# Sparse attention and MoE: fewer weight operations in the first stage, the gate's low part on GpSimd for one chunk, V's middle rows in one transfer

## The chip, the cores and the metric

The kernel runs on one core of a Trainium2 chip. The metric is the device time of one execution in microseconds. A core has TensorE (PE in the profile; PEld is its weight load), VectorE (DVE), ScalarE (ACT), GpSimd (POOL) and SyncE (SP, which only issues transfers here). SP, ACT and GpSimd each have a queue of transfers of their own; 16 DMA engines serve them all.

## The reference

```python
# q, k, v: (4, 8, 768, 64); blocks of 32 rows, 24 of them; 3 sampled blocks for each
scores = scale * np.matmul(q, k.transpose(0, 1, 3, 2))
mask = np.abs(blk_i - blk_j) <= 1
mask = mask | (blk_i == 0) | (blk_j == 0) | (blk_i == n_blocks - 1) | (blk_j == n_blocks - 1)
for qb in range(n_blocks):
    for kb in sampled_blocks[qb]:
        mask[qb * block:(qb + 1) * block, kb * block:(kb + 1) * block] = True
scores = np.where(mask, scores, -1000000000.0)
...
attn = attn / (np.sum(attn, axis=-1, keepdims=True) + 1e-09)
attn_out = np.matmul(attn, v)                  # then laid out as x: (3072, 512)
h = x @ w_in                                   # (512, 2048)
g = h * (1.0 / (1.0 + np.exp(-1.702 * h)))
out = g @ w_out                                # (2048, 512)
```

All of it is float32.

## The kernel before

**Units and items.** Queries are taken in units of 64 rows. For each batch the first and the last block form a dense unit (all 768 keys, two items of four heads each); the other 22 blocks form eleven sparse units, and a pair of batches shares their keys and values. A sparse unit needs its neighbour blocks, block 0, block 23 and three sampled blocks per query block. Its values lie in two tiles: `vown` (128 rows for each of the two query blocks, gathered by an indirect DMA that GpSimd issues, with row numbers in `vidx`) and `vmid` (64 rows of the two query blocks themselves, 64 rows of the blocks 0 and 23, loaded by SP; a row of both batches is 4,160 bytes). `vmidof` remembers the batch pair whose edge rows a buffer holds, so that later only the first 64 rows are loaded. Entries of V have an `at`, their buffer (four in the first stage, then two), and are loaded by `load_v` once the entry that held the buffer before has had all its values issued.

**Order.** Everything is written out by hand: `run` opens with loads, `first` works through the items of units 0 to 8, then come the ticks. Items 0 to 3 are dense, 4 and 5 sparse, 6 to 9 dense, 10 to 12 sparse. An item goes through scores (L344 dense, L334 sparse), maximum on DVE, exponentials on ACT, transposes (L383) with copies on ACT, values (L421 dense, L412 sparse), normalisation and a turn (L445) into `x`. `loads` is called at the end of each item and asks for as many keys and rows as have a free buffer. In this stage the keys of sparse units are copied by GpSimd from the resident `kres` (L245, L249).

**The sampled blocks.** `indices`, a generator, turns the sampled blocks into `vidx`. It loads them twice on ACT's queue: one row (`sbr`) and a copy on all 128 partitions.

**The weights.** `weights` is a generator too: it turns the 32 loads of 512 KB of 64-bit words (`raw`) into high and low float32r parts (`win`, `wout`). Two calls open it; then each block takes four calls: a shift on DVE (with the request for a load some blocks ahead), an and-or on DVE and an absolute value on ACT for the next block, the low part of the block before on DVE, an or on DVE and a cast on ACT. The blocks of `w_out` end with a 256 KB store to `ws`. The first stage makes some calls between items, `tick` makes the rest: n0 after the first part of the attention, n1 inside `gate`, n2 at the end.

**The MoE.** A chunk is 512 tokens (8 units), and a tick is one of 16 feature blocks of a chunk: `up` (12 matmuls, L576 to L578), `gate` (tanh on ACT, product on DVE), `gate_hi` (cast on ACT to float32r), `gate_lo` (the rest, g - ghi, on DVE, at the start of the next tick), `down` for the tick before (16 matmuls; L627 and L628 take `ghi`, L623 at the end takes `glo`). Ticks 0 to 15 are the first chunk; in them the rest of the weights is made and the attention of the next units goes on. At even ticks there are an item's scores, at odd ones its transposes.

Of the kernel before, what the change touches and what calls it, by code (L numbers as in the profile page):

```python
# [9 lines left out]
F32 = mybir.dt.float32  # L10
# [8 lines left out]
P = 128  # L19
# [35 lines left out]
class Kernel:  # L55
# [3 lines left out]

    def __init__(self, ctx, tc, q, qd, kb, kT, v, vd, sb, w_in, w_out, out):  # L60
        self.tc, self.nc = tc, tc.nc
        self.q, self.qd, self.kb, self.kT, self.v, self.vd, self.sb = q, qd, kb, kT, v, vd, sb
        self.w64, self.out = (w_in.bitcast(I32), w_out.bitcast(I32)), out
# [75 lines left out]
        self.knext = self.vnext = 0  # L139
        self.early = True  # L140

# [7 lines left out]
    def indices(self):  # L149
# [15 lines left out]

        sb_i = take([2 * NB * NR]).bitcast(I32).rearrange("p (a b c) -> p a b c", a=NB, b=NR)
        nc.scalar.dma_start(out=sb_i.rearrange("p a b c -> p (a b c)"), in_=sb32.partition_broadcast(P))
        sbw = sb_i[:, :, :, 0]

        vblk = take([NB])  # L170
# [14 lines left out]
        make_identity(nc, self.ident)  # L185
        yield
        nc.vector.memset(vblk[:, 0:NB:NB - 1], 0.0)
        rr = take([NB, NR])
        d = take([NB, NR])
        ok = take([NB, NR])  # L190
        ne = take([NB, NR])
        nc.vector.tensor_copy(out=rr, in_=sbw)
        nc.vector.tensor_tensor(out=d, in0=rr, in1=qb.rearrange("p (a b) -> p a b", b=1).broadcast_to([P, NB, NR]), op=ALU.subtract)
# [67 lines left out]
    def load_v(self, e):  # L261
        nc, b, u, r = self.nc, e["b"], e["u"], e["at"]
        if u is None:
# [3 lines left out]
            return  # L267
        q0, v = 2 * u + 1, self.v[b // 2]
        if self.vmidof[r] != b:
            for h in range(2):  # L270
                r0 = BLK * (NB - 1) * h
                nc.sync.dma_start(out=self.vmid[r][UT + BLK * h:UT + BLK * (h + 1)], in_=v[r0:r0 + BLK])
            self.vmidof[r] = b
        nc.sync.dma_start(out=self.vmid[r][0:UT], in_=v[BLK * q0:BLK * (q0 + 2)])
        for j in range(2):
# [4 lines left out]
    def loads(self):  # L280
# [10 lines left out]
        def rows():  # L291
            n = self.vnext
            behind = self.vent[n]["behind"] if n < len(self.vent) else None
            if n == len(self.vent) or behind is not None and behind["values"]:
                return False
            self.load_v(self.vent[n])
            self.vnext += 1
            return True
# [300 lines left out]
    def gate_lo(self, m):  # L599
        if m not in self.g or len(self.g[m]) != 2:  # L600
            return
        g, ghi = self.g[m]
        glo = self.work.tile([P, CT], F32R, name="glo")
        self.nc.vector.tensor_tensor(out=glo, in0=g, in1=ghi.bitcast(F32), op=ALU.subtract)  # L604
        self.g[m].append(glo)
# [107 lines left out]
    def tick(self, m):  # L713

        n0, n1, n2 = 0, 0, 0
        if m < NF:
            heavy = any(part == self.scores for q in range(QT) for part, g in self.at.get(QT * m + q, ()))
            n0, n1, n2 = (2, 2, 4) if heavy else (2, 2, 2)

# [205 lines left out]
    def first(self):  # L925
# [7 lines left out]
        def weights(k):  # L933
            for _ in range(k):
                next(self.conv)
# [10 lines left out]
        def opening():  # L946
            a, b, c = items[:3]
            (least, *exps), (more, *other) = self.scores(a), self.scores(b)
            finish([least])
# [24 lines left out]
        for n, g in enumerate(items):  # L974
# [11 lines left out]
            if not sparse:  # L986
                finish(exps)
            weights(1 if sparse else 2)
            values(n - 2)
# [3 lines left out]
            if n >= len(items) - 3:  # L993
                values(n - 1)
            weights(0 if sparse else 2 if n == 3 else 1)
            pending.append(g)
            self.flush()
            self.loads()
        finish(self.transposes(items[-1]))
        while turns:  # L1000
# [100 lines left out]
```

## Time and profile before

| | |
|---|---|
| time, median of 3 runs | 737.5 us (736.21 to 739.92) |
| profiled execution | 734.55 us, span 732.8 us |
| TensorE busy | 712.3 us (97%), mean granted clock 0.993 |
| DVE, ACT, GpSimd busy | 451.0, 387.9, 62.3 us |
| moved by DMA | 123.23 MB, 168 GB/s on average |

The span runs from the first to the last instruction on the core; the time is a little longer. Busy shares are averages over stages that differ, so they are to be read by stretch. The first matmul of the first tick (L576) starts at 77.65 us: what lies ahead of it is called the first stage below.

### The profile page before, as it was taken

The numbers are of one execution on the slowest core, as the hardware profiler recorded it, in microseconds if no ns is written. First come the engines' busy times: TensorE is split into PE (matmuls) and PEld (weight loads), VectorE is DVE, ScalarE is ACT, GpSimd is POOL, SyncE is SP. The second block draws the span as 40 slices with busy tenths as digits, with TensorE's granted clock in tenths as the row PEclk, the third lists the DMA queues.
The fourth block names the chain that finished last, engine by engine and source line by source line (L and its number), as shares of the span: only waits on it lengthen the run. The fifth ranks groups of instructions, "written<-read, shape, count | busy, mean of one in ns | idle before, by whom it ended". The sixth has DMA issues, their size and how long they took to land.

```text
span 732.8 us, 18738 instructions
## 1 busy us (share of the span) xinstructions
PE 712.3 (97%) x7552; PEld 561.8 (77%) x7552; DVE 451.0 (62%) x839; ACT 387.9 (53%) x759; POOL 62.3 (9%) x105
## 2 busy tenths in 40 slices
PE   7987999999999999999999999999999999999996
PEld 4655788787778777877777777778778788888885
DVE  4676898899644544554454444554577877676552
ACT  4776767767455445554454445544334564545442
POOL 2236001011001111111011111100000000000000
PEclk9999999999999999999999999999999999999999
DMA  8999678888476666667565646721111311011542
GB/s 326 370 367 302 200 262 275 263 261 290 137 232 198 190 182 194 189 188 213 160 188 177 191 133 189 220 72 31 44 44 43 87 29 44 30 43 30 144 116 72
DMA packets 58872, 123.23 MB, mean 168 GB/s; under 512 B 7137, under 2 KB 24930, under 8 KB 58786
## 3 DMA queue, kind: packets, MB, share of 16 engines
q1 hardware_dynamic: 44928, 76.91, 34.5%
q0 software_dynamic: 6336, 23.43, 10.0%
q10 hardware_dynamic: 7522, 21.70, 9.1%
q8 instruction: 59, 0.97, 0.6%
q14 instruction: 27, 0.22, 0.1%
HBM read 111.53 MB, written 10.49 MB: 167 GB/s over the span
## 4 chain that ended last, share of the span: by engine, by line
PE 86%; DMA 6%; DVE 4%; ACT 2%; issue 1%; SPq 0%; ACTq 0%
PE banks L623 12%; PE banks L627 11%; PE banks L628 11%; PE banks L839 10%; PE banks L576 8%; PE banks L577 7%; PE banks L578 7%; PE banks L412 6%; PE banks L334 6%; PE banks L383 5%; DMA vown<-in_v_dram,vidx 2%; DMA vmid<-in_v_dram 2%; DMA raw<-in_moe_w_in_dram 2%; PE banks L445 1%; PE banks L344 1%; DMA kres<-in_kT_dram 1%
## 5 line engine op out<-in xcount | busy, mean ns | idle before, releaser
L627 PE MATMUL banks<-wout,ghi 128*128 128x512 f32 x384 | 151.4, 394 | 0.0
L628 PE MATMUL banks<-wout,ghi 128*128 128x512 f32 x384 | 149.7, 390 | 0.0
L623 PE MATMUL banks<-wout,glo 128*128 128x512 f32 x384 | 107.6, 394 | 1.2 <-DVE glo L604 1.0
L365 ACT ACTIVATE ex<-banks,nm 128x256 f32<-128x256 f32 x176 | 69.0, 478 | 74.4 <-DVE rg L428 74.0
L565 DVE TENSOR_TENSOR wout<-wst,wout 128x512 fp32r<-128x512 f32 x80 | 55.2, 690 | 69.3 <-ACT wout L564 68.7
L584 ACT ACTIVATE g<-banks 128x512 f32<-128x512 f32 x64 | 38.3, 599 | 86.9 <-PE banks L578 86.8
L627 PEld LDWEIGHTS banks<-wout,ghi 128*128 128x128 f32 x384 | 72.1, 188 | 15.9 <-ACT ghi L596 0.6
L623 PEld LDWEIGHTS banks<-wout,glo 128*128 128x128 f32 x384 | 70.7, 188 | 17.3 <-DVE glo L604 2.6
L628 PEld LDWEIGHTS banks<-wout,ghi 128*128 128x128 f32 x384 | 72.1, 188 | 14.9 <-DVE wout L496 0.5
L576 PE MATMUL banks<-x,win 128*128 128x512 f32 x192 | 78.7, 410 | 0.1
L389 ACT COPY pt<-banks 128x512 f32<-128x512 f32 x112 | 61.2, 589 | 30.2 <-PE banks L383 26.9
L577 PE MATMUL banks<-x,win 128*128 128x512 f32 x192 | 75.1, 391 | 0.0
L578 PE MATMUL banks<-x,win 128*128 128x512 f32 x192 | 75.0, 391 | 0.0
L276 POOL DMA_INDIRECT vown<-in_v_dram,vidx x44 | 42.4, 963 | 376.4 <-PE banks L412 363.5
L591 DVE SCALAR_TENSOR_TENSOR g<-g,banks 128x512 f32<-128x512 f32 x51 | 35.0, 687 | 58.8 <-ACT g L584 58.6
L596 ACT CAST ghi<-g 128x512 fp32r<-128x512 f32 x80 | 50.1, 626 | 37.4 <-DVE g L591 31.3
L351 DVE TENSOR_REDUCE mx<-banks 128x4 f32<-128x1024 f32 x44 | 53.7, 1220 | 25.6 <-PE banks L334 25.6
L383 PEld LDWEIGHTS banks<-ident,ex 128*128 128x128 f32 x436 | 49.9, 141 | 15.2 <-ACT pt L389 4.7
L383 PE MATMUL banks<-ident,ex 128*128 128x128 f32 x436 | 58.4, 276 | 2.0 <-ACT pt L389 1.4
L412 PEld LDWEIGHTS banks<-vown,pt 128*32 128x32 f32 x1408 | 42.2, 109 | 19.9 <-issue 13.4
L564 ACT CAST wout<-wst 128x512 fp32r<-128x512 f32 x80 | 50.5, 631 | 10.4 <-DMA wst<-ws 8.5
L604 DVE TENSOR_TENSOR glo<-g,ghi 128x512 fp32r<-128x512 f32 x80 | 54.8, 685 | 0.7
(123 smaller groups left out, 1148.8 us busy)
## 6 DMA issues: line engine op xcount, KB each, us to landing
wst<-ws SPq DMA_DIRECT2D x80, 256.0 KB, 2.7
kg<-in_kb_dram SPq DMA_DIRECT2D x126, 128.0 KB, 2.8
raw<-in_moe_w_in_dram ACTq DMA_DIRECT2D x16, 512.0 KB, 9.6
raw<-in_moe_w_out_dram ACTq DMA_DIRECT2D x16, 512.0 KB, 8.0
kg<-in_kb_dram SPq DMA_DIRECT2D x18, 384.0 KB, 4.8
vown<-in_vd_dram SPq DMA_DIRECT2D x8, 780.0 KB, 11.8
vmid<-in_v_dram SPq DMA_DIRECT2D x22, 260.0 KB, 5.6
qt<-in_q_dram SPq DMA_DIRECT2D x22, 256.0 KB, 2.8
```

The lines of the kernel that those rows point to most:

```text
L365: nc.scalar.activation(out=ex[:, cols], in_=sps[h][:, cols], func=AF.Exp, bias=un["nm"][:, c:c + 1], scale=SCALE)
L383: self.nc.tensor.transpose(ps[:, slot], g["ex"][h][:, k * P:(k + 1) * P], self.ident)
L389: self.nc.scalar.copy(out=pt, in_=ps)
L412: nc.tensor.matmul(sums[BLK * c:BLK * (c + 1), 2 * i + h], g["pt"][h][:, 2 * i + k, BLK * c:BLK * (c + 1)], src[:, at:at + DV], start=(k = ...
L565: self.nc.vector.tensor_tensor(out=t[:, DM:2 * DM], in0=w, in1=t[:, 0:DM].bitcast(F32), op=ALU.subtract)
L576: nc.tensor.matmul(h, wih[:, k], hi[:, k], start=(k == 0), stop=False)
L577: nc.tensor.matmul(h, wih[:, k], lo[:, k], start=False, stop=False)
L578: nc.tensor.matmul(h, wil[:, k], hi[:, k], start=False, stop=(k == NCT - 1))
L623: nc.tensor.matmul(o[n], glo[:, tk[n]], woh, start=False, stop=last)
L627: nc.tensor.matmul(o[n], ghi[:, tk[n]], woh, start=(f == 0), stop=False)
L628: nc.tensor.matmul(o[n], ghi[:, tk[n]], wol, start=False, stop=False)
L839: self.nc.tensor.matmul(bank, a[:, k], b[:, k], start=start and k + n == 0, stop=k == 1 and n == 2, skip_group_check=True)
```

## The change

- `weights`: in `first`, dense items after item 3 make one call and not three; in the first chunk the ticks without scores make seven calls and not six.
- `gate_lo`: for the 16 feature blocks of the first chunk the subtraction is issued on GpSimd and not on DVE.
- `held`: in the first stage no rows of V from entry 11 (`NV3`) on are loaded until the loop over the items has ended.
- `vm`: a second layout of V in DRAM holds the 128 middle rows of each unit together; where the edge rows are wanted too, one transfer of 128 rows takes the place of three.
- `indices`: the copy of the sampled blocks on all partitions is no longer loaded; a matmul of a row of ones with the row of sampled blocks makes it in bank 7, and ACT copies it out. The generator has one step more, taken between the scores of the first two items.

```diff
--- before.py
+++ after.py
@@ -57,9 +57,9 @@
-    def __init__(self, ctx, tc, q, qd, kb, kT, v, vd, sb, w_in, w_out, out):
+    def __init__(self, ctx, tc, q, qd, kb, kT, v, vm, vd, sb, w_in, w_out, out):
         self.tc, self.nc = tc, tc.nc
-        self.q, self.qd, self.kb, self.kT, self.v, self.vd, self.sb = q, qd, kb, kT, v, vd, sb
+        self.q, self.qd, self.kb, self.kT, self.v, self.vm, self.vd, self.sb = q, qd, kb, kT, v, vm, vd, sb
         self.w64, self.out = (w_in.bitcast(I32), w_out.bitcast(I32)), out
         self.ctx = ctx
         pool = self.pool = lambda name, bufs, **k: ctx.enter_context(tc.tile_pool(name=name, bufs=bufs, **k))
@@ -137,7 +137,7 @@
             e["at"] = (0, 2, 1, 3)[n % 4] if n < NV3 else (n - NV3) % RING
             e["behind"] = next((o for o in reversed(self.vent[:n]) if o["at"] == e["at"]), None)
         self.knext = self.vnext = 0
-        self.early = True
+        self.early = self.held = True
@@ -163,10 +163,11 @@
             at[0] += n
             return flat.rearrange("p (a b) -> p a b", a=shape[0]) if len(shape) == 2 else flat
-        sb_i = take([2 * NB * NR]).bitcast(I32).rearrange("p (a b c) -> p a b c", a=NB, b=NR)
-        nc.scalar.dma_start(out=sb_i.rearrange("p a b c -> p (a b c)"), in_=sb32.partition_broadcast(P))
-        sbw = sb_i[:, :, :, 0]
-
+        rr, d, both = take([NB, NR]), take([NB, NR]), take([2 * NB * NR])
+        ok, ne = (both[:, NB * NR * k:NB * NR * (k + 1)].rearrange("p (a b) -> p a b", a=NB) for k in range(2))
+        ones = both[0:1, 0:P]
+        nc.gpsimd.memset(ones, 1.0)
+        nc.vector.tensor_copy(out=d[0:1], in_=self.sbr)
         vblk = take([NB])
         first, second = slice(1, NB - 2, 2), slice(2, NB - 1, 2)
         nc.gpsimd.iota(vblk[3 * BLK:P, first], pattern=[[2, NU]], base=-NB, channel_multiplier=0,
@@ -184,12 +185,11 @@
         self.ident = self.bits.tile([P, P], F32, name="ident")
         make_identity(nc, self.ident)
         yield
+        spread = self.bank[7][:, 0:NB * NR]
+        nc.tensor.matmul(spread, ones, d[0:1].rearrange("p a b -> p (a b)"), start=True, stop=True)
+        nc.scalar.copy(out=rr, in_=spread.rearrange("p (a b) -> p a b", a=NB))
+        yield
         nc.vector.memset(vblk[:, 0:NB:NB - 1], 0.0)
-        rr = take([NB, NR])
-        d = take([NB, NR])
-        ok = take([NB, NR])
-        ne = take([NB, NR])
-        nc.vector.tensor_copy(out=rr, in_=sbw)
         nc.vector.tensor_tensor(out=d, in0=rr, in1=qb.rearrange("p (a b) -> p a b", b=1).broadcast_to([P, NB, NR]), op=ALU.subtract)
         nc.vector.tensor_tensor(out=ne[:, :, 0:2], in0=rr[:, :, 0:2], in1=rr[:, :, 1:3], op=ALU.not_equal)
         nc.vector.tensor_tensor(out=ne[:, :, 2], in0=rr[:, :, 0], in1=rr[:, :, 2], op=ALU.not_equal)
@@ -265,13 +265,9 @@
             nc.sync.dma_start(out=flat, in_=self.vd[b, e["i"]])
             e["vd"] = flat.rearrange("p (h k a d) -> p h k a d", h=2, a=2, d=DV)
             return
-        q0, v = 2 * u + 1, self.v[b // 2]
-        if self.vmidof[r] != b:
-            for h in range(2):
-                r0 = BLK * (NB - 1) * h
-                nc.sync.dma_start(out=self.vmid[r][UT + BLK * h:UT + BLK * (h + 1)], in_=v[r0:r0 + BLK])
-            self.vmidof[r] = b
-        nc.sync.dma_start(out=self.vmid[r][0:UT], in_=v[BLK * q0:BLK * (q0 + 2)])
+        q0, rows = 2 * u + 1, P if self.vmidof[r] != b else UT
+        self.vmidof[r] = b
+        nc.sync.dma_start(out=self.vmid[r][0:rows], in_=self.vm[b // 2, u, 0:rows])
         for j in range(2):
             nc.gpsimd.indirect_dma_start(
                 out=self.vown[r][:, j], out_offset=None, in_=self.v.rearrange("b s c -> (b s) c"),
@@ -290,6 +286,8 @@
         def rows():
             n = self.vnext
+            if self.held and n >= NV3:
+                return False
             behind = self.vent[n]["behind"] if n < len(self.vent) else None
             if n == len(self.vent) or behind is not None and behind["values"]:
                 return False
@@ -601,7 +599,7 @@
             return
         g, ghi = self.g[m]
         glo = self.work.tile([P, CT], F32R, name="glo")
-        self.nc.vector.tensor_tensor(out=glo, in0=g, in1=ghi.bitcast(F32), op=ALU.subtract)
+        (self.nc.gpsimd if m < NF else self.nc.vector).tensor_tensor(out=glo, in0=g, in1=ghi.bitcast(F32), op=ALU.subtract)
         self.g[m].append(glo)
     def down(self, m, part):
@@ -715,7 +713,7 @@
         n0, n1, n2 = 0, 0, 0
         if m < NF:
             heavy = any(part == self.scores for q in range(QT) for part, g in self.at.get(QT * m + q, ()))
-            n0, n1, n2 = (2, 2, 4) if heavy else (2, 2, 2)
+            n0, n1, n2 = (2, 2, 4) if heavy else (2, 2, 3)
         def run(n):
             for _ in range(n):
@@ -945,7 +943,9 @@
         def opening():
             a, b, c = items[:3]
-            (least, *exps), (more, *other) = self.scores(a), self.scores(b)
+            least, *exps = self.scores(a)
+            next(self.index)
+            more, *other = self.scores(b)
             finish([least])
             finish(exps)
             finish([more])
@@ -985,17 +985,18 @@
                 copies.append(self.turned(before, 2))
             if not sparse:
                 finish(exps)
-            weights(1 if sparse else 2)
+            weights(1 if sparse or n > 3 else 2)
             values(n - 2)
             finish(copies)
             if sparse:
                 finish(exps)
             if n >= len(items) - 3:
                 values(n - 1)
-            weights(0 if sparse else 2 if n == 3 else 1)
+            weights(2 if n == 3 else 0)
             pending.append(g)
             self.flush()
             self.loads()
+        self.held = False
         finish(self.transposes(items[-1]))
         while turns:
             finish(self.turn(turns.pop(0)))
@@ -1076,6 +1077,13 @@
     vs[:, :S, :, :, :D] = v.reshape(2, 2, S, H, D).transpose(0, 2, 1, 3, 4)
     vs[:, :S, :, :, D] = 1.0
+    vm = _np.empty((2, NU, 2 * UT, 2 * VROW), _np.float32)
+    for u in range(NU):
+        vm[:, u, :UT] = vs.reshape(2, SV, 2 * VROW)[:, BLK * (2 * u + 1):BLK * (2 * u + 3)]
+    for h in range(2):
+        r0 = BLK * (NB - 1) * h
+        vm[:, :, UT + BLK * h:UT + BLK * (h + 1)] = vs.reshape(2, 1, SV, 2 * VROW)[:, :, r0:r0 + BLK]
+
     def words(w):
         return _np.ascontiguousarray(w).view(_np.int64).reshape(NF, P, DM)
@@ -1086,6 +1094,7 @@
         "in_kb_dram": _np.ascontiguousarray(kb).reshape(P, 2, NB, 2 * NPAIR * BLK),
         "in_kT_dram": _np.ascontiguousarray(kT).reshape(B, P, NPAIR * S),
         "in_v_dram": vs.reshape(2, SV, 2 * VROW),
+        "in_vm_dram": vm,
         "in_vd_dram": vd.reshape(B, 2, P, VDROW),
         "in_sampled_blocks_dram": _np.ascontiguousarray(inputs["sampled_blocks"]),
         "in_moe_w_in_dram": words(inputs["moe_w_in"].reshape(NCT, P, NF, P).transpose(2, 1, 0, 3)),
```

## Rows read from the trace of the kernel before

**Rows 1.** Stretches: length, then busy us (and instructions) of each engine, clock, DMA share, GB/s.

```profile
30.00:40.00 10.00, 7.38 (x182) 5.33 (x163) 6.25 (x13) 6.77 (x14) 1.14 (x3) 1.00 1.03 315
...
40.00:50.00 10.00, 9.96 (x132) 6.04 (x132) 8.26 (x18) 6.23 (x12) 3.54 (x9) 0.83 1.03 414
...
60.00:70.00 10.00, 6.68 (x187) 4.96 (x183) 5.09 (x11) 5.01 (x12) 6.74 (x14) 1.00 1.03 265
...
77.65:192.00 114.35, 114.24 (x1230) 90.72 (x1230) 102.05 (x195) 78.13 (x156) 8.16 (x8) 1.00 0.80 253
192.00:520.00 328.00, 328.00 (x4241) 258.75 (x4240) 160.60 (x316) 160.57 (x347) 26.29 (x28) 1.00 0.57 171
```

**Rows 2.** What TensorE waited for from 0 to 75 us: total, times, longest.

```profile
PE banks L412 <- DMA vmid<-in_v_dram: 2.6, 1, 2.6
PE banks L344 <- DMA kres<-in_kT_dram: 2.4, 2, 2.1
PE banks L412 <- DMA vown<-in_v_dram,vidx: 1.8, 1, 1.8
...
PE banks L334 <- issue: 1.0, 1, 1.0
```

**Rows 3.** The chain that ended last, from 0 to 200 us: start, length, what.

```profile
25.93 12.87 DMA vmid<-in_v_dram
...
40.04 2.71 PE banks L344 x16
...
46.10 1.85 PE banks L344 x16
...
52.67 14.77 DMA vown<-in_v_dram,vidx
...
77.65 0.43 PE banks L576
...
115.19 0.91 PE banks L623 x4
```

**Rows 4.** Stretches, columns as in the first group, behind two of the waits.

```profile
40.00:44.00 4.00, 4.00 (x27) 2.08 (x26) 2.44 (x7) 1.00 (x3) 1.20 (x4) 0.57 1.04 415
66.00:68.00 2.00, 0.51 (x36) 0.51 (x40) 1.39 (x3) 1.65 (x5) 1.37 (x4) 1.00 1.05 272
```

**Rows 5.** Timeline of ACT and its queue: start, length, engine and line.

```profile
51.62 1.04 ACTq L478 DMA_DIRECT2D raw<-in_moe_w_out_dram  x1
...
56.92 0.33 ACTq L478 DMA_DIRECT2D raw<-in_moe_w_in_dram  x1
```

**Rows 6.** Timeline of GpSimd in the first stage.

```profile
53.61 2.66 POOL L245 COPY kg<-kres 128x256 f32<-128x256 f32 x6
...
62.04 0.94 POOL L276 DMA_INDIRECT vown<-in_v_dram,vidx  x1 [0.69 <-PE banks L421]
```

**Rows 7.** Timeline of SP's issues in the first stage.

```profile
23.31 2.58 SPq L272 DMA_DIRECT2D vmid<-in_v_dram  x2
```

**Rows 8.** The page's transfers: line, issues, KB each, median us from issue to landing.

```profile
wst<-ws SPq DMA_DIRECT2D x80, 256.0 KB, 2.7
...
vmid<-in_v_dram SPq DMA_DIRECT2D x22, 260.0 KB, 5.6
```

**Rows 9.** The page's groups: the low part on DVE, busy us and mean ns.

```profile
L604 DVE TENSOR_TENSOR glo<-g,ghi 128x512 fp32r<-128x512 f32 x80 | 54.8, 685 | 0.7
```

**Rows 10.** Timeline of ACT in the first chunk.

```profile
111.05 0.61 ACT L596 CAST ghi<-g 128x512 fp32r<-128x512 f32 x1
```

**Rows 11.** Timeline of DVE in the first stage.

```profile
55.14 0.87 DVE L496 TENSOR_TENSOR wout<-a,wout 128x512 fp32r<-128x512 f32 x1
...
65.35 1.01 DVE L353 TENSOR_SCALAR nm<-mx 128x4 f32<-128x4 f32 x1
```

**Rows 12.** Waits of all engines from 77 to 195 us.

```profile
ACT a L488 <- DMA raw<-in_moe_w_in_dram: 8.0, 6, 2.2
```

## The prediction

> **What bounds the kernel now.** I first read the stretches [rows 1]. From 77.65 us on, through the first chunk of the MoE and far beyond it, TensorE is busy without a gap (114.24 of 114.35 us, then 328.00 of 328.00): time can be won there by nothing but less TensorE work, and the change takes none away. Ahead of 77.65 us lies the attention stage, and its rows look different: DMA share 1.03 in each of the three stretches shown, TensorE busy only 7.38 of 10 us at 30 to 40 and 6.68 at 60 to 70, and a granted clock of 0.83 at 40 to 50. So the first 77 us are set by the transfers, the rest by TensorE.
>
> Next, TensorE's waits in that stage [rows 2]: 2.6 us for `vmid`, 2.4 us for `kres`, 1.8 us for the gathered `vown`, 1.0 us put to nothing ("issue"). The chain that ended last [rows 3] shows `vmid` and the gather from the other side: the last `vmid` transfer of the first sparse pair takes 12.87 us from issue to landing, and a gather 14.77 us, although each is a fraction of a megabyte. They are long because everything shares the 16 engines.
>
> A stall has a second price. Behind the 2.6 us wait the clock is 0.57 over 4 us [rows 4], so for most of them at the lower of its levels, 1.2 and not 2.4 GHz: the score matmuls of one item take 2.71 us there against 1.85 us a little later [rows 3]. That is (1 - 0.57) x 4 = 1.7 us of lost work. Around the 1.8 us wait, in which TensorE is busy 0.51 of 2 us, the clock stays at 1.00 [rows 4].
>
> **The change, part by part.**
>
> *Weight operations.* `weights` is a generator; two calls open it, then four make one weight block. The first stage now makes 1 call in the opening, 4 at item 3, 1 each at items 4 and 5, 1 each at items 6 to 9 (was 3 each), 1 each at items 10 to 12: 14 instead of 22. A block's load is asked for three blocks ahead in this stage, so 14 calls ask for 6 loads where 22 asked for 8. The two that leave the stage are those issued at 51.62 and 56.92 us [rows 5], 0.52 MB each; the one before them slides down by three items, because block 2 now begins at item 9, and the 0.26 MB store of `ws` that ends this block moves to item 12. So from 45 to 67 us the ACT queue carries some 1.3 MB less. Nothing changes before 45 us.
>
> *`held`.* The rows of entry 11 of V, two gathers, the first issued at 62.04 us [rows 6], and 64 rows of `vmid`, now wait until the loop over the items has ended. They are needed only at tick 4, some 28 us (4 x 114.35 / 16) into the first chunk, so the delay itself costs nothing; what they gave up is DMA time in the same stretch (rows are 4,160 bytes: 2 x 128 and 64 of them, 1.06 + 0.27 MB). No queue is held up by them: on GpSimd the key copies that came behind them come earlier.
>
> *V's middle rows.* Where a buffer first serves a batch pair, three transfers on SP (32, 32 and 64 partitions) become one of 128; the bytes are the same. SP was at the first two from 23.31 to 25.89 us [rows 7], and issued the third at 25.93 [rows 3]. In a backlogged queue an earlier issue alone wins nothing, since the bytes ahead are the same; what could win is the shape: 260 KB on 64 partitions land after a median 5.6 us, 256 KB of `wst` on 128 partitions after 2.7 us [rows 8]. So the landing at 38.80 us comes between 0 and 2.9 us earlier. I take 1.3 us, near the middle, as part of the 5.6 us is the queue and not the shape. The stall of 2.6 us becomes 1.3 us, shorter than the 1.8 us one that left the clock alone, so I also take the 1.7 us of clock as won; both may be nothing.
>
> *The sampled blocks.* A 72 KB broadcast load on ACT is replaced by one matmul with K = 1 and 72 columns, one ACT copy and a DVE cast of one row. The matmul goes between the first two items' scores, where TensorE waits up to 2.1 us for `kres` anyway [rows 2]; that wait is its cover, and without it it would cost some tenths of a us, once. The 72 KB at the 414 GB/s of 40 to 50 us [rows 1] are 0.2 us, which I take off the `kres` wait, with 0 and 0.5 us as bounds (small pieces may cost more than their bytes).
>
> *The gather's wait.* The 14.77 us gather [rows 3] starts when TensorE has left its buffer (the values of entry 5), so if TensorE comes 3 us earlier, so does the gather, and it must be through in 14.77 - 1.8 = 12.9 us to cause no wait. Against it ran the two weight loads, the store and later entry 11: the 22 us from 45 to 67 us carry 5.8 to 9.1 MB at the 265 to 414 GB/s of [rows 1]; without 1.3 to 2.6 MB of them, a seventh to two fifths, 14.77 us become 9 to 12.7. I take the 1.8 us as won. The 1.0 us "issue" [rows 2] may go too, but nothing shows what it waits for; I count none of it, and all of it for the upper bound.
>
> *The gate's low part.* Sixteen subtractions of 128x512 leave DVE, 685 ns each [rows 9], 11.0 us. GpSimd has no such row; a copy of 256 columns takes it some 0.44 us (2.66 us for six) [rows 6], so 512 columns are 0.8 to 0.9 us by columns, and twice that, 1.6 to 1.8 us, if the second input costs as much as the first. I take 1.6 us, bounds 0.8 and 2.0. TensorE needs the result at the end of the next tick: in one of the tighter ticks `ghi` is ready at 111.05 + 0.61 = 111.66 us [rows 10] and the low matmuls begin at 115.19 us [rows 3], so there are 3.5 us, and 1.6 us fit. GpSimd's queue holds only gathers beside it; `gate_lo` is issued ahead of the tick's gather, so it never stands behind a gather that waits for that tick's values.
>
> *DVE in the first chunk.* It is busy 102.05 of 114.35 us [rows 1]. Off: 11.0 us. On: the eight calls, two blocks of four operations of 512 columns at the same 0.69 us, 5.5 us. On top: what GpSimd's reads do to DVE operations with two SBUF inputs. While GpSimd copied [rows 6], such a subtraction took 0.87 us at 55.14 us [rows 11] in place of 0.685 [rows 9]: 0.185 us per copy of 0.44 us, so 16 x 1.6 x 0.185 / 0.44 = 10.8 us. Together 107.3 us, still under 114.35: no cost. Bounds: nothing, and the whole GpSimd time, 16 x 1.6 = 25.6 us, below as a rival. The Trainium skill, "SBUF — State Buffer", section "SBUF: two separate sides", says that the port pair which GpSimd shares with DVE is an exclusive lock, held for a whole instruction, against DVE operations with two SBUF inputs too. By that rule DVE would stand for each whole subtraction; the row above shows a partial delay. The same skill, "GPSIMD Engine Reference", section 3.1, gives 2.6 cycles per element at 1.2 GHz for two inputs; 512 elements would be an estimated 1.1 us, less than what I take.
>
> *Lead of the weights.* A tick pair now makes 8 + 7 calls (was 8 + 6), so 14 + 8 x 15 = 134 = 22 + 8 x 14: both end the chunk level. A block is ready four calls or more before the matmul that reads it, two for `wout` at the last ticks, as before; at tick 8 the lead falls from 11 calls to 7. No cost. ACT takes two blocks more in the chunk, 78.13 of 114.35 us now [rows 1], no bound.
>
> **Sum.** 1.3 (stall for `vmid`) + 1.7 (clock) + 1.8 (gather) + 0.2 (`kres`) = 5.0 us; bounds 0 and 2.6 + 1.7 + 2.8 + 0.5 = 7.6 us. The profiled execution took 734.55 us (span 732.8 and 1.75 around it), which becomes 729.6. It is 3 us under the median of the three runs, 737.5, for which the time is 732.5 us.
>
> **The rivals.**
>
> *The relief is hidden.* The first 45 us of transfers are the same bytes, so the `vmid` stall may stay, and with it the clock: then only 1.8 + 0.2 us come, perhaps less where another wait takes the gather's place: 735.5 to 737. For it: DMA share 1.03 at 30 to 40 us [rows 1]. Against it: the narrow transfers of `vmid` land late for their size [rows 8]. Chance 0.30.
>
> *ACT stalls in the first chunk.* Two weight loads more are asked for there. ACT already waits for `raw` in the chunk, 8.0 us in 6 waits, the longest 2.2 us [rows 12], and TensorE doesn't feel it. If two more such waits came at a bad place and passed through to TensorE, 4.4 us of the 5.0 would go: 736.9. Chance 0.06.
>
> *DVE becomes the bound (slower).* Should a GpSimd subtraction stop DVE for its whole length g, DVE's work is 102.05 - 11.0 + 5.5 + 16 g. It passes 114.35 us at g = 1.11 us; it eats the 5.0 us at g = 1.42; at g = 2.0 the chunk is 14.2 us longer, and the time is 737.5 - 5.0 + 14.2 = 746.7 us. For it: beside GpSimd's copies an operation on four columns took DVE 1.01 us [rows 11]. Against it: the 0.185 us above. Chance 0.08. By the rule of "SBUF — State Buffer" named above this is the case to expect; only the partial delay of the row keeps its chance low.
>
> **How the numbers follow.** The forecast (a gain of 3.7 to 7.6 us) has 0.56. A measurement of this kernel can tell about 0.5% from no change, 3.7 us. Faster 0.56; same 0.30 + 0.06 = 0.36; slower 0.08. For 8 in 10 the range runs from 729.0 (8.5 us won, the bound and some 1 us for what one measurement differs from the next) to 738.0: it leaves out the slower rival and a few hundredths at the lower end.
>
> **What would show it.** Right: the first up-projection begins near 72.7 us instead of 77.65; TensorE's wait for `vmid` is under 1.8 us and the clock at 40 to 44 us is 1.00; no wait for the gather; the chunk behind stays about 114.3 us long, with TensorE gapless and DVE near 107 us. Wrong: the wait for `vmid` and the low clock are still there, or a new wait stands at another item of the first stage; a GpSimd subtraction over 3.5 us, or a DVE without idle time and TensorE waiting for `glo`, `g` or `wout`.

## The result, and the profile after

The changed kernel takes 743.08 us (median of 10 runs, 741.32 to 745.80), the kernel before 736.38 us (median of 10 runs): 1.0088 times as long, 95% interval 1.0069 to 1.0106. It is slower by 0.9%; forecast was 732.5 us in a range of 729.0 to 738.0.

The stretches say where the time went. Columns as in [rows 1]; the first fence is the changed kernel, cut at its first up-projection (72.25 us) and at the one of tick 16, the second the kernel before, cut at the same places of the program.

```profile
0.00:72.25 72.25, 62.97 (x1194) 45.29 (x1194) 44.68 (x109) 47.44 (x88) 27.07 (x70) 1.00 0.88 331
72.25:198.02 125.77, 117.18 (x1227) 89.75 (x1221) 106.67 (x182) 80.38 (x159) 30.84 (x24) 0.99 0.72 238
198.02:740.50 542.48, 534.46 (x5146) 427.55 (x5140) 301.23 (x534) 260.65 (x513) 26.23 (x28) 1.00 0.42 128
```

```profile
77.65:190.00 112.35, 112.24 (x1222) 89.05 (x1221) 100.16 (x190) 77.76 (x155) 8.16 (x8) 1.00 0.80 255
190.00:732.80 542.80, 534.50 (x5141) 427.15 (x5140) 301.08 (x534) 260.64 (x513) 26.29 (x28) 1.00 0.43 128
```

The first stage is 77.65 - 72.25 = 5.4 us shorter (5.3 by the timeline of TensorE, in which the first matmul of the kernel before starts at 77.58), the forecast was 5.0. The rest behind the first chunk is the same (542.48 and 542.80). The first chunk, forecast unchanged, is 125.77 us long instead of 112.35: 13.4 us more. In 8.6 of them TensorE is idle (125.77 - 117.18); it is also busy for 4.9 us more, of which some 1.5 are the low clock shown below (0.50 over 3 us) and the others were not traced. What it waits for there, in the second fence, it did not wait for before; the first fence is the first stage and answers to [rows 2].

```profile
PE banks L381 <- ACT pt L387: 2.4, 5, 0.9
PE banks L342 <- DMA kres<-in_kT_dram: 1.7, 3, 0.8
PE banks L342 <- ACT ex L366: 1.2, 1, 1.2
...
PE banks L410 <- DMA vmid<-in_vm_dram: 0.6, 1, 0.6
```

```profile
PE banks L626 <- DVE wout L494: 5.0, 4, 1.8
PE banks L381 <- ACT ex L363: 2.9, 1, 2.9
PE banks L576 <- DVE win L494: 0.2, 1, 0.2
```

In the first stage the wait for `vmid` fell from 2.6 to 0.6 us, the one for the gather is gone, and the clock stands at 1.00 over the whole stage, at 40 to 44 us too (first row below), where [rows 4] had 0.57. In the chunk there are two kinds of wait. One is late weights: the second matmul of a down-projection (L626) wants the low half of `wout`, and DVE has not made it. The other is a single stall of 2.9 us, in front of the transposes of tick 5, with the clock at 0.50 behind it (second row).

```profile
40.00:44.00 4.00, 2.75 (x83) 1.74 (x83) 2.08 (x8) 2.46 (x4) 1.87 (x5) 1.00 1.01 413
```

```profile
109.00:112.00 3.00, 3.00 (x9) 2.27 (x8) 2.73 (x4) 2.69 (x7) 1.37 (x1) 0.50 0.37 112
```

What stands ahead of the single stall is in ACT's timeline (start, length, engine and line, and the idle time before it): a load of weights is asked for at 98.52 us, ACT stands still for 3.95 us for it, and behind that operation in its queue are the exponentials (L363) that the transposes need.

```profile
98.52 0.39 ACTq L476 DMA_DIRECT2D raw<-in_moe_w_in_dram  x1
...
106.00 0.72 ACT L486 ACTIVATE a<-raw 128x512 f32<-128x512 f32 x1 [3.95 <-DMA raw<-in_moe_w_in_dram]
106.57 0.51 ACT L363 ACTIVATE ex<-banks,nm 128x256 f32<-128x256 f32 x1
```

The kernel before has such a load at the same tick, asked for at 103.06 us and used 7.4 us later, after ACT has stood still for 1.75 us. There the exponentials (L365) are ahead of the operation that waits, and TensorE doesn't feel it. The view puts the end of that wait down to a transfer of keys, so the load itself may have landed a little earlier.

```profile
103.06 0.34 ACTq L478 DMA_DIRECT2D raw<-in_moe_w_in_dram  x1
...
106.20 1.57 ACT L365 ACTIVATE ex<-banks,nm 128x256 f32<-128x256 f32 x4 [1.38 <-DVE rg L428]
...
110.48 0.67 ACT L488 ACTIVATE a<-raw 128x512 f32<-128x512 f32 x1 [1.75 <-DMA kg<-in_kb_dram]
```

The last view is of GpSimd and DVE around two of the moved subtractions. DVE's shift of 512 columns (L524) takes 0.42 us as a rule; beside GpSimd's subtraction it takes 1.36 us, and it ends some 0.3 us after GpSimd does (110.63 + 1.61 = 112.24; 111.17 + 1.36 = 112.53). The other subtractions look alike: wherever a shift began beside one, it ended 0.28 to 0.29 us after GpSimd, and a subtraction of DVE's own ended 0.55 us after it.

```profile
110.63 1.61 POOL L602 TENSOR_TENSOR glo<-g,ghi 128x512 fp32r<-128x512 f32 x1 [8.29 <-ACT ghi L594]
117.18 1.62 POOL L602 TENSOR_TENSOR glo<-g,ghi 128x512 fp32r<-128x512 f32 x1 [4.94 <-ACT ghi L594]
```

```profile
111.17 1.36 DVE L524 TENSOR_SCALAR a<-a 128x512 int32<-128x512 int32 x1
...
114.71 0.42 DVE L524 TENSOR_SCALAR a<-a 128x512 int32<-128x512 int32 x1
...
117.73 1.36 DVE L524 TENSOR_SCALAR a<-a 128x512 int32<-128x512 int32 x1
```

### The profile page after: what moved, and what is told of

The parts are those of the page before. It is cut to its first block, busy times and chain, and to the rows that moved or that the text cites. A ratio compares the mean times of both kernels' runs of the same rounds, so it can differ in the third digit from the quotient of the medians.

```text
span 740.5 us, 18757 instructions
## 1 busy us (share of the span) xinstructions
PE 714.6 (97%) x7554; PEld 562.6 (76%) x7554; DVE 452.6 (61%) x823; ACT 388.5 (52%) x760; POOL 84.1 (11%) x122
## 4 chain that ended last, share of the span: by engine, by line
PE 68%; DVE 4%; ACT 3%; issue 1%; DMA 1%; ACTq 0%
PE banks L621 10%; PE banks L625 9%; PE banks L837 9%; PE banks L626 9%; PE banks L574 6%; PE banks L575 5%; PE banks L576 5%; PE banks L410 5%; PE banks L332 4%; PE banks L381 4%; PE banks L443 1%; DVE gs L760 1%; DMA raw<-in_moe_w_in_dram 1%; ACT ghi L594 1%; DVE wout L563 1%
## 5 line engine op out<-in xcount | busy, mean ns | idle before, releaser
L626 PE MATMUL banks<-wout,ghi 128*128 128x512 f32 x384 | 150.4, 392 | 5.1 <-DVE wout L494 5.0
L363 ACT ACTIVATE ex<-banks,nm 128x256 f32<-128x256 f32 x176 | 69.0, 479 | 78.0 <-DVE rg L426 53.9
L626 PEld LDWEIGHTS banks<-wout,ghi 128*128 128x128 f32 x384 | 72.2, 188 | 21.8 <-DVE wout L494 7.4
L625 PEld LDWEIGHTS banks<-wout,ghi 128*128 128x128 f32 x384 | 72.1, 188 | 15.7 <-ACT ghi L594 0.4
L349 DVE TENSOR_REDUCE mx<-banks 128x4 f32<-128x1024 f32 x44 | 53.7, 1220 | 24.4 <-PE banks L332 24.3
L410 PE MATMUL banks<-vown,pt 128*32 128x65 f32 x1408 | 50.3, 221 | 1.9 <-ACT pt L387 1.0
```

The lines of the kernel that those rows point to most:

```text
L363: nc.scalar.activation(out=ex[:, cols], in_=sps[h][:, cols], func=AF.Exp, bias=un["nm"][:, c:c + 1], scale=SCALE)
L410: nc.tensor.matmul(sums[BLK * c:BLK * (c + 1), 2 * i + h], g["pt"][h][:, 2 * i + k, BLK * c:BLK * (c + 1)], src[:, at:at + DV], start=(k = ...
L625: nc.tensor.matmul(o[n], ghi[:, tk[n]], woh, start=(f == 0), stop=False)
L626: nc.tensor.matmul(o[n], ghi[:, tk[n]], wol, start=False, stop=False)
```

## The experiments

All times are medians, against runs of the kernel before on the same chip. "Calls" are the weight calls of the first stage and of a tick pair; "low part" is the engine of the gate's subtraction in the first chunk; the last three columns are read from each trace's timeline of TensorE: the start of the first up-projection, the length of the first chunk from there to tick 16 (112.35 us in the kernel before), and the longest distance between the scores (32 matmuls) of two even ticks up to tick 14, which is 14.3 us in the kernel before. The pair of ticks 14 and 15, 14.3 to 18.7 us long, is left out of that column. The runs e1 to e4 were made on one chip, e5, e6, e8 and e9 on a second, e7 and e10 to e12 on a third, e13 and e14 on a fourth.

| kernel | calls | low part | us | before | ratio (95%) | first tick | chunk | longest pair |
|---|---|---|---|---|---|---|---|---|
| the change | 14, 15 | GpSimd | 743.08 | 736.38 | 1.0088 (1.0069 to 1.0106) | 72.25 | 125.77 | 19.8 |
| e1_lo_dve | 14, 15 | DVE | 739.93 | 737.26 | 1.0038 (1.0018 to 1.0058) | 72.49 | 122.00 | 18.6 |
| e2_weights_old | 22, 14 | GpSimd | 730.53 | 737.26 | 0.9899 (0.9879 to 0.9918) | 72.34 | 114.20 | 15.8 |
| e3_both_undone | 22, 14 | DVE | 730.20 | 737.26 | 0.9898 (0.9879 to 0.9916) | 72.45 | 112.92 | 14.3 |
| e4_before_lo_pool | 22, 14 | GpSimd | 736.71 | 737.26 | 0.9989 (0.9976 to 1.0002) | 78.38 | 113.27 | 15.2 |
| e5_first18 | 18, 15 | DVE | 733.83 | 737.31 | 0.9962 (0.9940 to 0.9985) | 71.24 | 119.28 | 15.9 |
| e6_first22_15 | 22, 15 | DVE | 735.19 | 737.31 | 0.9964 (0.9945 to 0.9983) | 70.14 | 123.63 | 20.0 |
| e8_exps_first | 14, 15 | DVE | 746.69 | 737.31 | 1.0128 (1.0095 to 1.0162) | 69.71 | 132.32 | 20.9 |
| e9_first14_16 | 14, 16 | DVE | 731.03 | 737.31 | 0.9915 (0.9886 to 0.9945) | 69.81 | 117.02 | 15.8 |
| e12_change_16 | 14, 16 | GpSimd | 734.11 | 737.07 | 0.9962 (0.9948 to 0.9976) | 70.36 | 120.52 | 15.9 |
| e13_noloads14 | 14, 15 | DVE | 733.33 | 738.18 | 0.9933 (0.9906 to 0.9959) | 70.30 | 118.90 | 16.2 |
| e14_noloads22 | 22, 15 | DVE | 729.90 | 738.18 | 0.9890 (0.9864 to 0.9916) | 69.84 | 115.64 | 15.5 |
| e7_vm_only | 22, 14 | DVE | 730.86 | 737.07 | 0.9915 (0.9899 to 0.9932) | 73.35 | 114.86 | 15.5 |
| e10_held_only | 22, 14 | DVE | 735.94 | 737.07 | 0.9992 (0.9978 to 1.0007) | 77.22 | 112.05 | 14.3 |
| e11_index_only | 22, 14 | DVE | 736.63 | 737.07 | 0.9992 (0.9977 to 1.0007) | 76.36 | 114.86 | 14.6 |

**The two parts that touch the chunk, each alone and both undone.** Theory LOCK blames GpSimd's subtractions, theory LEAD the moved weight calls.

e1_lo_dve:

```diff
-        (self.nc.gpsimd if m < NF else self.nc.vector).tensor_tensor(out=glo, ...)
+        self.nc.vector.tensor_tensor(out=glo, ...)
```

> The changed kernel with the gate's low part back on DVE; the eight weight calls stay in the first chunk. Theory LOCK (a GpSimd subtraction stops DVE's operation beside it until it is done, and the weights come late by that): the first chunk falls from 125.8 us back to 113 to 116 us, the first stage stays near 72.3 us, so the time is about 12 us under the changed kernel, 729 to 733 us, below the kernel before. Theory LEAD (the eight moved calls alone leave the weights too little lead, and ACT waits for their loads): DVE has 11 us more to do here, the chunk stays at 122 us or more, the time at 740 to 748 us.

e2_weights_old:

```diff
-            n0, n1, n2 = (2, 2, 4) if heavy else (2, 2, 3)
+            n0, n1, n2 = (2, 2, 4) if heavy else (2, 2, 2)
...
-            weights(1 if sparse or n > 3 else 2)
+            weights(1 if sparse else 2)
...
-            weights(2 if n == 3 else 0)
+            weights(0 if sparse else 2 if n == 3 else 1)
```

> The changed kernel with the weight calls of the kernel before (22 in the first stage, 8 and 6 in the tick pairs); the low part stays on GpSimd. LOCK: DVE is stopped as often as in the changed kernel, so its operations beside GpSimd still take 1.0 to 1.6 us and the chunk stays near 120 us or more: 736 to 742 us. LEAD: the weights have their old lead of 15 calls, which hides the stops: the chunk is 112 to 115 us, the first stage between 72.3 and 77.7 us: 731 to 736 us.

e3_both_undone has both diffs.

> Both undone; what stays of the change is V's middle rows in one transfer, the held rows and the sampled blocks by a matmul. Both theories: the chunk is that of the kernel before, 112 to 114 us. What it tells is where the first stage's 5.4 us came from: if from the wider transfer and the opening, it stays under 74 us and the time is 731 to 734 us; if from the two weight loads less, it goes back to 76 to 78 us and the time to 735 to 737 us.

e4_before_lo_pool is the kernel before with the first diff turned round (DVE to GpSimd).

> The kernel before with nothing changed but the low part of the first chunk on GpSimd. LOCK alone: the chunk grows by several us, 740 to 748 us in all. LEAD: the old lead hides it, the time is that of the kernel before within 2 us.

LOCK as the main cause fell: with the low part back on DVE the kernel is still slower than the one before, and with the weight calls back it is 1.0% faster, whichever engine does the low part (e2, e3); on the kernel before GpSimd's part can't be told from nothing (e4). The moved calls cost 739.93 - 730.20 = 9.7 us. GpSimd adds some 3 us, but only where they have been moved (743.08 against 739.93). And the moved calls bought nothing: on the chip of e1 to e4 the first tick starts at 72.49 us with 14 calls (e1) and at 72.45 us with 22 (e3), on the second chip at 69.71 and 69.81 us with 14 (e8, e9) and at 70.14 us with 22 (e6), on the fourth at 70.30 and 69.84 us (e13, e14). Between these groups the same first stage differs by up to 2.8 us. Whether that is the chip was not tested; but a difference between medians from two chips can hold as much that has nothing to do with the edit, so the chunks are compared beside them below.

**Lead in microseconds.** From the timelines one can read when DVE ended the low half of `wout` of a feature block and when TensorE came to the down-projection that reads it. The second matmul of a down-projection is the first that wants the low half; without a wait it starts 0.23 us after the first one. From DVE's end to that moment, in us (negative: TensorE waited):

```
feature block    0     2     4     6     8    10    12    13    14
before         28.8  11.6   9.9   5.4   5.5   3.3   2.2  -0.1   0.5
e3  (22, 14)   27.2  11.6   9.6   5.4   4.5   3.3   1.1  -0.7   0.5
the change      4.3   2.2   3.1   0.6  -0.6  -1.5   0.2  -0.3  -1.5
e1  (14, 15)    4.3   2.7   3.0   1.9   0.5  -0.9   0.5  -0.2  -1.2
e9  (14, 16)    4.3   3.6   3.4   3.4   3.4   3.4   3.4   4.8   4.4
e6  (22, 15)   25.8  11.6  13.9  11.5   8.7   7.8   4.5   7.1   5.7
```

The kernel before runs its lead down to zero just at block 13: it had none to give away. With eight calls less zero is reached at block 8 (the change) or 10 (e1), and from there on TensorE goes at the pace of the weights. One such wait, in TensorE's timeline of the changed kernel:

```profile
169.77 0.50 PE L626 MATMUL banks<-wout,ghi 128*128 128x512 f32 x1 [1.77 <-DVE wout L494]
```

The next four kernels vary the lead, and try to take away the long pair at ticks 4 and 5.

e5_first18 is e1 with `weights(0 if sparse else 2 if n == 3 else 1)` at the end of an item, so one call more in each of four items.

> Low part on DVE, 18 weight calls in the first stage (two in each dense item after item 3), 15 in a tick pair. LEAD in us: a call of lead is worth about 1 us; 14 calls (e1) ran out of slack at tick 8 to 10, 22 calls (e3) at tick 13; 18 with 15 a pair keep a lead of 8 or 9 calls, so TensorE doesn't wait for wout: 730 to 733 us. A rival, RATE (15 calls a tick pair are more than DVE and ACT can do, whatever the lead): tick pairs of 15 us and more from about tick 6 on, 735 to 740 us.

e6_first22_15 is e3 with `(2, 2, 4) if heavy else (2, 2, 3)`, one call more in a tick pair.

> Low part on DVE, 22 weight calls in the first stage, and 15 in a tick pair, one more than the kernel before has. LEAD: never short, 729 to 731 us, as with 22 and 14 or up to 0.6 us better. RATE: the pairs are too full, 733 to 738 us.

e9_first14_16 is e1 with:

```diff
-            n0, n1, n2 = (2, 2, 4) if heavy else (2, 2, 3)
+            n0, n1, n2 = (2, 2, 4)
```

> Low part on DVE, 14 weight calls in the first stage as in the change, and 16 in a tick pair, so that the lead stays at some 8 calls and doesn't fall to 2. LEAD: the late ticks don't wait for wout any more; what is left is the stall at ticks 4 and 5 by a load: 733 to 736 us. RATE: 16 calls are worse than 15, 739 to 745 us.

e8_exps_first is e1 with:

```diff
-        if not turning:
+        if not turning and not (m < NF and heavy):
             self.flush()
```

> The changed kernel with the low part on DVE (739.9 us), and in the ticks with scores the weights' ACT operations left over from the tick before come behind the exponentials and not ahead of them. If the tick pair of 18.6 us (ticks 4 and 5) comes from ACT standing at an absolute value that waits for its load, with the exponentials behind it (theory RAW, beside LEAD): this pair falls to 14.3 to 15 us, the later ones stay long, 735 to 737 us. If the pair is long for want of lead: no change, 738 to 741 us.

With 16 calls in a pair the slack stays at 3.4 us or more, no `wout` is late, and the time is 731.03 us: LEAD holds. The stall that was expected to stay at ticks 4 and 5 did not come: that pair is 15.7 us long. RATE as it was put, 739 to 745 us, falls, since the densest pairs are the best of the three kernels with 14 calls. But fuller pairs are not free: e9's chunk is 117.02 us long where e3's is 112.92, and the two times agree only because e9's first tick, on the other chip, starts 2.6 us earlier. In e5, which was expected at 730 to 733 us and takes 733.83, no `wout` is late either; its TensorE waits for `g`, DVE's product, in the last ticks (first fence). And e6 was expected at 729 to 731 us and takes 735.19: it has slack in plenty, waits for `g` too, and still has one pair of 20.0 us. So LEAD isn't all. e6's TensorE and ACT show the same stall as the changed kernel, at the same place (second and third fence):

```profile
PE banks L574 <- DVE g L589: 2.9, 2, 1.6
```

```profile
PE banks L381 <- ACT ex L363: 2.7, 1, 2.7
PE banks L574 <- DVE g L589: 2.4, 2, 1.3
```

```profile
97.56 0.39 ACTq L476 DMA_DIRECT2D raw<-in_moe_w_in_dram  x1
...
104.90 0.67 ACT L486 ACTIVATE a<-raw 128x512 f32<-128x512 f32 x1 [3.83 <-DMA raw<-in_moe_w_in_dram]
105.47 0.46 ACT L363 ACTIVATE ex<-banks,nm 128x256 f32<-128x256 f32 x1
```

e8 was a miss: it shortened that pair only from 18.6 to 16.6 us, and, as the weights' ACT operations now came later, TensorE waited for the high half of `wout` too. At 746.69 us it is the slowest of all.

```profile
PE banks L625 <- ACT wout L501: 3.9, 2, 3.1
PE banks L626 <- DVE wout L494: 3.6, 4, 2.4
PE banks L574 <- ACT wst L587: 2.3, 2, 1.2
```

**Is it the loads?** In e13 and e14 no weights are loaded behind the first stage:

```diff
                 f, i = todo[k]
+                if not self.early:
+                    tiles[k] = {"raw": tiles[4 + k % 2]["raw"]}
+                    return
```

> Low part on DVE, 14 calls in the first stage, 15 in a tick pair (739.9 us), but after the first stage the weights' loads are left out: the later blocks are made again from two tiles that are already there, so the weights are wrong and 26 loads of 512 KB are missing. Two causes are told apart. If the long tick pair 4 and 5 (18.6 us) is ACT waiting for a load, it falls to 14.3 to 15 us, while the late ticks still wait for wout (lead): 734 to 736.5 us. If the pair is long for want of lead, it stays above 17 us, and the time within 2 us of 739.9. If the waits for wout too come from the loads, all goes: under 732 us.

> The same omission with 22 calls in the first stage and 15 in a tick pair (735.2 us; 24 loads missing, wrong weights). This kernel has lead enough, and one long pair, 20.0 us at ticks 4 and 5. If this is the load: all pairs near 14.3 us and 728 to 731 us. If it is where 15 calls a pair fall in the tick, whatever they wait for: it stays, 734 us or more.

Without loads the pair at ticks 4 and 5 is 14.8 us long in e13 and 14.7 us in e14. e14, which has its lead, is at 729.90 us, 5.3 us under e6. e13, which hasn't, is at 733.33 us, 6.6 us under e1, and its waits for `wout` stay:

```profile
PE banks L629 <- DVE wout L497: 3.7, 3, 1.5
PE banks L381 <- ACT ex L363: 0.3, 1, 0.3
```

So there are two losses, and taking away the loads leaves the other. The lead's size can be read off on one chip: 733.33 - 729.90 = 3.4 us, and 118.90 - 115.64 = 3.3 us by the chunks. That of the late loads is less sure. By medians it is 6.6 us, but e13 ran on another chip than e1, and in the two traces 2.2 us lie ahead of the first tick, where the kernels are the same; by the chunks it is 122.00 - 118.90 = 3.1 us, which is what the stall itself comes to: the wait for the exponentials falls from 2.1 to 0.3 us, and 1.4 us of clock (0.72 over 5 us in e1, from 108 us on) come back. From e14's chunk to e3's another 115.64 - 112.92 = 2.7 us are left, with neither loads nor a short lead: what remains of the edit there is the fifteenth call in each pair. That is no more than two traces can differ by: e7 and e11 have the weight calls of the kernel before and chunks 2.5 us longer.

**The first stage, part by part, on the kernel before.** e7_vm_only has the diff's lines of `vm` and no others, e10_held_only those of `held`, e11_index_only those of `indices` and the `next(self.index)` between the first scores.

> The kernel before with V's middle rows in one transfer and nothing else. Of the first stage's some 5 us that stay when the weight calls go back (e3), the wider transfer should bring the wait for vmid (2.6 us) and the low clock behind it (1.7 us): the first stage ends 3 to 4.5 us earlier, 732.5 to 734.5 us. If the rival holds that the landing is set by the bytes ahead of it in the queue: 736 to 738 us.

> The kernel before with the rows of V from entry 11 on held back, and nothing else. If the gather's wait of 1.8 us came from these rows: 735 to 736 us; if from the other transfers: no change, 737 us.

> The kernel before with the sampled blocks spread by a matmul instead of a 72 KB load, and nothing else. By the prediction 0.2 us; if the low clock of 8 to 14 us goes with a shorter wait for kres (it is 1.00 in the changed kernel's first 20 us, 0.86 at 10 to 20 us before), 1.5 to 2.5 us: 735 to 736 us.

The one wide transfer alone brings 6.2 us. `held` and the sampled blocks alone can't be told from nothing; in both the wait for `vmid` stands (e11 in the first fence), and the second fence is what is left of it in e7. The gather's wait is gone in e7 and in e10, so either part alone ends it; in e11 it is 1.4 us.

```profile
PE banks L412 <- DMA vmid<-in_v_dram: 3.5, 1, 3.5
PE banks L344 <- DMA kres<-in_kT_dram: 1.7, 3, 0.8
```

```profile
PE banks L340 <- DMA kres<-in_kT_dram: 3.2, 2, 2.4
...
PE banks L408 <- DMA vmid<-in_vm_dram: 0.9, 1, 0.9
```

The wide transfer does more than land earlier: from 30 to 40 us the DMA engines are as full as in the kernel before, but move 412 GB/s (below) where [rows 1] has 315; e4, e10 and e11, with the three narrow transfers, have 302 to 318. Whether the partitions do it or the number of transfers was not told apart: SP also issues the last `vmid` transfer 25.93 - 23.31 = 2.6 us earlier by it.

```profile
30.00:40.00 10.00, 9.08 (x169) 6.31 (x168) 7.92 (x18) 6.84 (x14) 1.84 (x6) 1.00 1.03 412
```

e11 has the shorter wait for `kres` (1.7 us in three pieces, the longest 0.8, where [rows 2] has 2.4 and 2.1), and nothing comes of it as long as `vmid` is waited for behind it: its wait is 3.5 us here.

**The change with one figure altered.** e12_change_16 is the changed kernel with e9's diff.

> The changed kernel with one figure more: 16 weight calls in every tick pair and not 15 (the low part stays on GpSimd). LEAD: as with the low part on DVE (731.0 us) the lead stays at some 8 calls, and the waits for wout go: 730 to 734 us, 9 us or more under the changed kernel. LOCK: GpSimd's subtractions still stop DVE 16 times, and the chunk has one call more in each pair: 738 us or more.

734.11 us: 9 us better than the change and 3.1 us worse than e9, which differs only in the engine of the low part. That lies between what LEAD (up to 734) and LOCK (from 738) gave. TensorE waits for no weights in it. DVE is busy 109.80 of 120.52 us in its chunk (first fence), no larger share than e9's 105.94 of 117.02, and TensorE's waits there for `g` are 2.1 us (second fence) where e9 has 0.7 (third). They explain 1.4 of the 3.1 us at most, and they are not GpSimd's alone, as e5 and e6 have more of them with the low part on DVE.

```profile
70.36:190.88 120.52, 116.07 (x1227) 88.83 (x1221) 109.80 (x183) 80.66 (x159) 32.28 (x24) 1.00 0.76 251
```

```profile
PE banks L574 <- DVE g L589: 2.1, 2, 1.1
```

```profile
PE banks L574 <- DVE g L589: 0.7, 1, 0.7
```

The best kernels are e3, e2, e7 and e9, at 730.2 to 731.0 us, which can't be told apart (e2 and e3 ran on one chip, e7 and e9 on two others); e7 is the smallest step from the kernel before. e14 is not among them, as it leaves loads out.

## Why the prediction was wrong

**The first stage: size right, source wrong.** 5.4 us came where 5.0 were worked out, as near as one trace of each can tell; by the medians of e3 it is 737.26 - 730.20 = 7.1 us, so how near is in part luck. The term for `vmid` was 1.3 and measured 2.0 (2.6 to 0.6 us; 1.7 in e7, with nothing else changed); the 1.7 us of clock came whole, though the length of the stall, from which I took it, doesn't decide it (in e8 the clock falls behind waits of 0.5 and 1.2 us). The sum had only the wait in it, and not that the three narrow transfers held the rate of a full queue down, 315 GB/s against 412. The gather's 1.8 us came too, but not by the weight calls, the first of the parts that I gave them to: with all 22 in the stage (e3) that wait is gone as well, and the first tick starts at the same 72.45 us. Two weight loads less, 1.3 MB, were worth nothing there. Part of what was won went to longer and new waits for ACT (2.4 us where it was 1.4, and 1.2 us, both above).

**The step that failed** is "Lead of the weights ... No cost." I counted the lead in calls (from 11 to 7 at tick 8, two for `wout` at the last ticks "as before") and called it enough because so few had caused no wait before. What counts is the time between DVE's end and TensorE's need. Counted in the same way for the low half of `wout`, the lead is five calls at block 8 of the changed kernel. In the kernel before the time had shrunk to 2.2 us at block 12, also at a lead of five calls, and to 0.5 us and less at the last blocks, at a lead of three; so five calls are worth very little, and to be down to them at block 8 instead of 12 makes half of the chunk go at the pace of the weights. The rows to see it were in the trace of before. The moved calls cost 9.7 us where I wrote "No cost"; 3.4 of them are this lead, and the late loads of the next paragraph are between half and all of the rest.

**The rival with 0.06** was right in mechanism, place and nearly in size: ACT waits for a load, passes the wait on to the exponentials, TensorE stands for 2.9 us, and the clock drops. I priced it at 4.4 us; leaving the loads out gave back 6.6 by medians and 3.1 by the chunks. Its chance was too low because the total of ACT's waits for loads barely changed in my reckoning; not the total decides but what is queued behind the one that is late. The load at 98.52 us took 7.4 us, no longer than there are between request and use of the one at this tick before; what changed between the two timelines is that the exponentials now stand behind the operation that waits for it. Why 18 calls at 15 a pair (e5) meet a milder form (15.6 us for the pair) was not settled.

**DVE.** Its busy time was forecast at 107.3 us over 114.35 us, which is 105.5 in the chunk as cut here, and is 106.67; a subtraction on GpSimd was put at 1.6 us and takes 1.42 on average. The mistake was the sentence behind it, "still under 114.35: no cost". A busy share under one doesn't make delays free. Where DVE has the old 14 calls in a pair the cost is nothing that the times show (e2 against e3, e4 against before; 1.3 and 0.9 us by the chunks); where it has 15 or 16 it is some 3 us (the change against e1, e12 against e9). By which way it reaches TensorE is not shown: TensorE's waits for `wout` grow by only 0.9 us in the one (5.0 against 4.1) and those for `g` by 1.4 in the other.

**The rival in which DVE stops** had its mechanism right as far as the single operation goes: beside a subtraction of 1.61 us the shift took 1.36 us and ended 0.3 us after it, so it had waited for nearly all of GpSimd's rest (0.94 of 1.07 us). The partial delay that I read from [rows 11] was beside copies only 0.4 us long, of which no more than a part was left to wait for. The trace agrees with the rule of the Trainium skill, "SBUF — State Buffer", section "SBUF: two separate sides", that a GpSimd operation holds the shared ports until its end. The price was not the one I gave that rival, as DVE was not full: 106.67 - (100.16 - 11.0 + 5.5) = 12.0 us of delay, 0.75 us for each subtraction, of which the time shows 3.

Put together, by medians: 7.1 us won (e3), 9.7 us lost by the moved calls (3.4 of it lead, 3 to 7 loads), some 3 us lost by GpSimd on top. That is a loss of some 6 us, and 6.7 lie between 736.4 and 743.1.

## What to carry to other kernels

Work that is made just ahead of its use has a slack in microseconds, and it is to be read as one: for each piece, the end of its last producer against the start of its reader, from the first to the last. If the last pieces have none, calls moved out of the stage ahead are paid for unless more are made on the way (e9), even though no wait shows before the change. And before a transfer-bound stage is relieved of bytes, find the one transfer that TensorE waits for: making one wide transfer of that one's three was worth 6.2 us, taking away 1.3 MB beside it nothing.

## What the runs showed of the hardware

- One transfer to all 128 partitions in place of three to 32, 32 and 64 (e7, nothing else changed) took the wait for it from 2.6 to 0.9 us at the same bytes, and the rate from 30 to 40 us from 315 to 412 GB/s at a DMA share of 1.03 in both.
- The granted clock fell to its lower level behind stalls of 2.6 us (kernel before, 40 us: 0.57), 2.1 us (before, 9.4 to 12.7 us: 0.50) and 2.9 us (after, 109 us: 0.50), and stayed at 1.00 behind 1.8 us (before, 67 us) and behind 2.4 us (e7, 9 us). In e8 it fell behind two of only 0.5 and 1.2 us (0.50 from 138 to 140 us). So the length of one stall alone doesn't tell it.
- GpSimd's subtraction of 128x512 takes 1.28 to 1.62 us; a DVE operation on SBUF that began beside it took up to 1.56 us instead of 0.68. A reduction that reads from PSUM (L349) took 1.22 us beside it (e2) as it does without (1.22 on average in the kernel before).
